# A four-batch fp32 chain of linear attention and two mixers: sign and low part of the weights by piece, the second batch's gates in the opening, the last output tile in halves

## The chip, the cores and the metric

The kernel runs on one core of a Trainium2 chip. Its engines work side by side, each through its own queue in program order: TensorE (PE, with its weight loads PEld), VectorE (DVE), ScalarE (ACT), GpSimd (POOL) and SyncE (SP), which issues nearly all DMAs. The metric is the device time of one execution in microseconds (us); lower is better. Of several runs the median is given.

## The reference

Attention with a decaying state, for 4 batches, 8 heads, 768 steps and a head dimension of 48; then a low-rank token mixer with a channel MLP; then a mixer with cosine and sine gates:

```python
f = 1.0 / (1.0 + np.exp(-f_logit))
for t in range(S):
    state = f[:, :, t, :, None] * state + einsum('bhd,bhe->bhde', k[:, :, t], v[:, :, t])
    y[:, :, t] = einsum('bhd,bhde->bhe', q[:, :, t], state)
x = y.transpose(0, 2, 1, 3).reshape(B, S, 384)
u = x + (x.transpose(0, 2, 1) @ U @ V).transpose(0, 2, 1)
x = u + np.maximum(u @ w_ch1, 0.0) @ w_ch2          # 384 -> 1536 -> 384
theta = x @ w_theta
y = einsum('ts,bsd->btd', w_tok_r, x * cos(theta)) + einsum('ts,bsd->btd', w_tok_i, x * sin(theta))
u = x + y
out = u + np.maximum(u @ w_ch, 0.0)
```

The weights come as float64 and the rest as float32.

## The kernel before

**Stages.** The program has an *opening* (about 0 to 55 us in the profile), which computes the attention of batch 0 in six chunks of 128 steps while the first weights arrive. Then `moe1(0)` runs batch 0's channel MLP, with the attention of batch 1 and the rest of the weights laid between its matmuls; `moe1(1)` and `moe1(2)` do the same with batches 2 and 3 and no more weights; `moe1(3)` is run with the conversion of the second mixer's weights; the second mixer (`theta`, `tok`, `chan`) ends the program.

**Matmuls in hi and lo.** An fp32 operand is kept as a rounded high part and the rest, and a product is three matmuls: hi by hi, hi by lo, lo by hi. `w1g(th, f)` (L630) computes 128 hidden features for one half of the tokens, nine matmuls; ScalarE then writes `hh` (L635) and VectorE `hl` (L636). `w2g(th, f)` (L647, L650) adds their product with the second weight into three PSUM banks `acc`; on a group's last feature block VectorE adds `acc` to `xT` (L655), and the next group's first `w2g` needs these banks back. In batch 0 the groups of feature blocks are `G0`: 0 to 1, 2 to 3, 4 to 7, 8 to 11, each for both token halves.

**Weights.** A weight piece is 128 x 768 numbers. It is loaded as float64 words into a buffer (`fetch`), and ScalarE's `scale` takes three steps: exponent byte (L995), sign (L998), mantissa and scale (L999). `join` (L1006) on VectorE puts them together; without `signs` VectorE takes the sign in one more operation (L1003). `w_store` then has ScalarE write the high part and GpSimd the low part (`split`, L184 and L181). The 14 pieces are numbered: 0 is U, 1 is V, then halves of w_ch1 and w_ch2 in turn (2 and 4 hold w_ch1 and 3 and 5 w_ch2 for feature blocks 0 to 3; 6 to 9 the same for 4 to 7; 10 to 13 for 8 to 11).

**Attention.** For a chunk, ScalarE takes the sigmoid of the gates (`pre_a`), VectorE runs a scan backward and one forward (`pre_s`, `pre_f`; L282, L295), and GpSimd multiplies k and q by them (L287, L299). TensorE transposes k (`kt`, L329), with a copy `ktok` on ScalarE (L331), and computes scores (`sc` in the opening, `sc4`, L384, for later batches), outputs (`xx`, copied to `xf` by ScalarE, L356) and the state (`kv`). `au` (L555) gathers the low-rank product, and on the last chunk ScalarE and VectorE make `as_` of it (L560 to L562). `first_x` and `first_h` (L591, L595) form batch 0's `u` in three PSUM banks, of which `uh` and `ul` are made.

**What sets the order.** `place` merges a list of main steps, each with a weight, with steps that have a position written as a fraction of the main list's total (1.0 and above: the first MLP stage). The positions stand in tables: `WPOS` (four steps of each weight piece: load, scale, join, store), `A1` and `A2` (the attention steps of batches 1 and 2/3), `NPOS` and `PPOS` (the second mixer's weights and first gates), `W0` (weights of the opening's steps). `KEEP` and `WARM` count matmuls on constant data (`keep_warm`, L548, 320 columns) that fill TensorE's idle time.

Of the kernel before, what the change touches and what calls it, by code (L numbers as in the profile page):

```python
# [35 lines left out]
NPOS = (
    (0.0277, 0.068, 0.0754, 0.1024),
    (0.0385, 0.1276, 0.1524, 0.178),
    (0.0319, 0.0967, 0.0975, 0.1909),
    (0.1497, 0.1976, 0.1984, 0.2572),  # L40
    (0.1837, 0.216, 0.2219, 0.2605),
    (0.234, 0.2743, 0.2753, 0.2992),
    (0.1972, 0.272, 0.2899, 0.3422),
    (0.2581, 0.3095, 0.3299, 0.3456),
    (0.2876, 0.3435, 0.36, 0.4385),
    (0.319, 0.3906, 0.3923, 0.4406),
    (0.3478, 0.4354, 0.4416, 0.4643),
    (0.3903, 0.4603, 0.4889, 0.5445),
    (0.4754, 0.5519, 0.5719, 0.5998),
    (0.4583, 0.5806, 0.5875, 0.6175),  # L50
    (0.5021, 0.5721, 0.5927, 0.6584),
    (0.5487, 0.6166, 0.6451, 0.7283),
    (0.6045, 0.66, 0.6659, 0.7498),
    (0.6183, 0.6617, 0.7209, 0.7603),
    (0.6784, 0.754, 0.7684, 0.9255),
    (0.7599, 0.7679, 0.8745, 0.9399),
    (0.7623, 0.8599, 0.8768, 0.9459),
    (0.8323, 0.9015, 0.9233, 0.9787),
    (0.9315, 0.9828, 0.9928, 1.022),
    (0.9407, 0.9937, 1.004, 1.124),  # L60
    (0.9513, 0.9992, 1.0067, 1.188),
    (1.0037, 1.0053, 1.0971, 1.1821),
    (1.0475, 1.07, 1.1124, 1.3954),
    (1.1245, 1.2045, 1.2545, 1.4229),
    (1.2775, 1.3859, 1.4334, 1.5908),
    (1.3022, 1.3332, 1.4535, 1.6135),
)
PPOS = (0.3153, 0.3907, 0.4483, 0.4725, 0.5134, 0.5728, 0.6238, 0.7426, 0.7666, 0.7963, 0.8271)
# [2 lines left out]
WPOS = (
    (0.1696, 0.231, 0.3752, 0.3979),
    (0.2201, 0.3286, 0.5165, 0.547),
    (0.2359, 0.4203, 0.7847, 0.7956),
    (0.4234, 0.6633, 0.8571, 0.9747),
    (0.2874, 0.9233, 1.0401, 1.0657),
    (0.5364, 0.9547, 1.0623, 1.1063),
    (0.4931, 1.0442, 1.1351, 1.1713),
    (0.5855, 1.1024, 1.1536, 1.2068),
    (0.7627, 1.1904, 1.2335, 1.279),  # L80
    (0.9717, 1.2212, 1.3155, 1.3293),
    (1.0728, 1.2667, 1.3516, 1.4777),
    (1.2008, 1.3522, 1.4323, 1.4924),
    (1.2548, 1.4587, 1.5342, 1.5986),
    (1.3056, 1.5483, 1.5725, 1.7332),
)
# [2 lines left out]
A1 = (
    (0.9797, 0.9861, 1.0081, 1.0804, 1.1072, 1.1676),  # L90
    (1.0384, 1.0515, 1.0971, 1.1995, 1.3043),
    (1.0862, 1.1911, 1.218, 1.3331, 1.4271),
    (1.3302, 1.348, 1.3792, 1.5171, 1.6043),
    (1.3769, 1.4457, 1.4633, 1.6201, 1.7007),
    (1.6233, 1.6281, 1.6693, 1.7973, 1.8787, 1.9131),
)
# [1125 lines left out]
```

## Time and profile before

| | us |
|---|---|
| median of 3 runs (693.7 to 695.59) | 694.93 |
| the profiled execution | 694.42 |
| its span on the core | 692.6 |
| TensorE busy | 666.1 (96%) |
| ScalarE busy | 346.9 (50%) |
| VectorE busy | 333.6 (48%) |
| GpSimd busy | 284.1 (41%) |

The rows of the trace are counted from the start of the span; the 1.8 us between span and time lie around it. A busy time is a sum over an engine's instructions in the trace. A row of the timeline gives start, duration, engine, line of the kernel, operation, tiles and shapes, and, in brackets, the idle time before it with what ended it. The granted clock is the share of full speed that TensorE was given: 1.00 is 2.4 GHz, 0.50 is 1.2 GHz.

### The profile page before, as it was taken

How to read it: one execution, taken by the hardware profiler on the slowest of the kernel's cores; microseconds unless marked ns; L12 is line 12 of the kernel's file. 1: busy time of each engine (PE TensorE's matmuls, PEld its weight loads, DVE VectorE, ACT ScalarE, POOL GpSimd, SP SyncE). 2: the span in 40 equal slices, each digit the busy share in tenths (PEclk: the TensorE clock that was granted, in tenths of full speed). 3: DMA queues.
4: the chain of work that ended last, by engine and by line, in shares of the span. 5: the costliest groups of instructions: out<-in, count | busy, mean ns of one | idle time of the engine just before them, and what ended most of it. 6: DMA issues, size and time to landing. Idle time of an engine off the chain costs nothing.

```text
span 692.6 us, 14789 instructions
## 1 busy us (share of the span) xinstructions
PE 666.1 (96%) x6196; PEld 639.5 (92%) x6196; DVE 333.6 (48%) x556; ACT 346.9 (50%) x702; POOL 284.1 (41%) x274
## 2 busy tenths in 40 slices
PE   8998989999999999999999999999999999999996
PEld 7767878998999998999999998999899999999996
DVE  7736766535534326435214678963543343343222
ACT  5868886634334234334223577766564364455321
POOL 6425757424624204534202235435572263235222
PEclk9998999999999999999999999999999999999999
DMA  9961443222222420223000444332000000000002
GB/s 243 317 194 59 131 124 101 59 59 59 58 59 72 99 61 1 59 59 81 2 1 1 128 145 138 92 115 69 2 1 35 35 0 24 35 12 13 34 24 74
DMA packets 20586, 49.79 MB, mean 72 GB/s; under 512 B 2496, under 2 KB 11200, under 8 KB 20512
## 3 DMA queue, kind: packets, MB, share of 16 engines
q1 hardware_dynamic: 20400, 48.38, 24.2%
q8 instruction: 51, 0.84, 0.5%
q10 hardware_dynamic: 112, 0.39, 0.2%
q14 instruction: 23, 0.19, 0.1%
HBM read 44.04 MB, written 4.72 MB: 70 GB/s over the span
## 4 chain that ended last, share of the span: by engine, by line
PE 67%; ACT 13%; DVE 6%; issue 5%; DMA 4%; POOL 3%; SPq 0%; POOLq 0%; ACTq 0%; DVEq 0%
PE ps_A L779 18%; PE ps_A L630 15%; PE ps_A L647 9%; PE ps_B L807 5%; PE ps_A L650 4%; PE ps_B L726 4%; DMA r<-in_wtok_dram 3%; PE ps_A L384 2%; ACT xT L998 2%; ACT w L998 1%; PE ps_B L407 1%; PE ps_B L436 1%; PE ps_B L430 1%; ACT W L184 1%; POOL W L181 1%
## 5 line engine op out<-in xcount | busy, mean ns | idle before, releaser
L636 DVE SCALAR_TENSOR_TENSOR hl<-ps_A,hh 128x384 fp32r<-128x384 f32 x96 | 53.1, 554 | 157.4 <-ACT hh L635 157.3
L779 PE MATMUL ps_A<-W,zh 128*128 128x384 f32 x576 | 125.1, 338 | 0.0
L647 PE MATMUL ps_A<-hh,W 128*128 128x384 f32 x552 | 115.8, 339 | 4.2 <-DVE xT L655 3.9
L630 PE MATMUL ps_A<-uh,W 128*128 128x384 f32 x576 | 119.2, 341 | 0.7 <-ACT uh L599 0.6
L635 ACT ACTIVATE hh<-ps_A 128x384 fp32r<-128x384 f32 x96 | 46.8, 489 | 122.8 <-PE ps_A L630 122.3
L630 PEld LDWEIGHTS ps_A<-uh,W 128*128 128x128 f32 x576 | 102.1, 191 | 2.4 <-ACT uh L599 1.1
L647 PEld LDWEIGHTS ps_A<-hh,W 128*128 128x128 f32 x552 | 96.0, 188 | 7.7 <-ACT w L995 2.9
L779 PEld LDWEIGHTS ps_A<-W,zh 128*128 128x128 f32 x576 | 100.7, 188 | 0.0
L181 POOL TENSOR_TENSOR zl<-z,zh 128x768 fp32r<-128x768 f32 x24 | 44.6, 1860 | 98.2 <-ACT zh L756 53.5
L779 PE MATMUL ps_A<-W,zl 128*128 128x384 f32 x288 | 73.3, 335 | 0.0
L630 PE MATMUL ps_A<-ul,W 128*128 128x384 f32 x288 | 66.3, 337 | 0.2 <-POOL ul L181 0.2
L650 PE MATMUL ps_A<-hl,W 128*128 128x384 f32 x276 | 65.8, 337 | 0.0
L181 POOL TENSOR_TENSOR ul<-xT,uh 128x384 fp32r<-128x384 f32 x45 | 47.1, 1060 | 42.8 <-ACT uh L580 26.4
L287 POOL TENSOR_TENSOR raw<-raw,e 112x512 f32<-112x512 f32 x24 | 32.1, 1338 | 57.4 <-DVE e L282 40.6
L630 PEld LDWEIGHTS ps_A<-ul,W 128*128 128x128 f32 x288 | 51.9, 190 | 0.7 <-POOL ul L181 0.7
L779 PEld LDWEIGHTS ps_A<-W,zl 128*128 128x128 f32 x288 | 52.1, 188 | 0.0
L650 PEld LDWEIGHTS ps_A<-hl,W 128*128 128x128 f32 x276 | 49.7, 188 | 0.1
L181 POOL TENSOR_TENSOR W<-r,W 128x384 fp32r<-128x384 f32 x24 | 27.0, 1138 | 39.9 <-ACT W L184 39.9
L732 DVE SCALAR_TENSOR_TENSOR ps_B<-kk,ps_B 128x384 f32<-128x384 f32 x24 | 13.5, 563 | 60.1 <-ACT kk L731 60.0
L181 POOL TENSOR_TENSOR xlo<-xf,xhi 128x384 fp32r<-128x384 f32 x18 | 18.3, 1014 | 58.8 <-ACT xhi L443 58.8
L299 POOL TENSOR_TENSOR raw<-raw,f 112x512 f32<-112x512 f32 x23 | 30.2, 1312 | 20.0 <-DVE f L295 17.3
L737 ACT ACTIVATE cs<-r 128x384 f32<-128x384 f32 x24 | 12.6, 525 | 42.3 <-DVE r L734 42.3
(201 smaller groups left out, 1186.4 us busy)
## 6 DMA issues: line engine op xcount, KB each, us to landing
raw<-in_qkf_dram SPq DMA_DIRECT2D x23, 576.0 KB, 5.2
r<-in_wtok_dram SPq DMA_DIRECT2D x24, 384.0 KB, 3.3
vt<-in_v_dram SPq DMA_DIRECT2D x24, 192.0 KB, 5.6
w<-in_w_dram SPq DMA_DIRECT2D x6, 768.0 KB, 8.2
xT<-in_w_dram SPq DMA_DIRECT2D x6, 768.0 KB, 5.6
out_dram<-o SPq DMA_DIRECT2D x24, 192.0 KB, 1.9
vt<-in_v_dram SPq DMA_DIRECT2D x36, 96.0 KB, 5.0
r<-in_wth_dram SPq DMA_DIRECT2D x3, 384.0 KB, 3.8
```

The source lines that it names most:

```text
L181: eng.tensor_tensor(out=out_, in0=a, in1=b, op=ALU.subtract)
L287: nc.gpsimd.tensor_tensor(out=x, in0=x, in1=e, op=ALU.mult)
L299: (nc.gpsimd if g else nc.vector).tensor_tensor(out=x, in0=x, in1=p, op=ALU.mult)
L630: mm(out=t, lhsT=w1t(lo, fb)[:, k, 128 * fo:128 * fo + 128], rhs=x[:, k], start=(n == 0), stop=(n == 8))
L635: nc.scalar.activation(out=hh, in_=t, func=ACTF.Relu)
L636: nc.vector.scalar_tensor_tensor(out=hl, in0=t, scalar=0.0, in1=f32(hh), op0=ALU.max, op1=ALU.subtract)
L647: mm(out=st["acc"][k], lhsT=w2t(lo, fb)[:, fo, 128 * k:128 * k + 128], rhs=hh, start=(first_of(f) and lo == 0), stop=False)
L650: mm(out=st["acc"][k], lhsT=w2t(0, fb)[:, fo, 128 * k:128 * k + 128], rhs=hl, start=False, stop=last_of(f))
L726: mm(out=t, lhsT=x[:, k], rhs=w[:, k], start=(n == 0), stop=(n == 8))
L779: mm(out=t, lhsT=z[:, i, 128 * k:128 * k + 128], rhs=w[:, S * i + HT * th:S * i + HT * th + HT], start=(s == 0 and n == 0), stop=(s == NCH ...
L807: mm(out=t, lhsT=w[:, k, 128 * m:128 * m + 128], rhs=x[:, k], start=(n == 0), stop=(n == 8))
L998: nc.scalar.activation(out=sign, in_=hi.bitcast(F32), func=ACTF.Copy, scale=2.0 ** -60)
```

## The change

Each weight piece gets an entry in `SIGNS`. Its lowest bit says whether ScalarE takes the sign (as before) or VectorE; the next bit puts the low part on VectorE instead of GpSimd. Pieces 2, 3, 4, 9 and 12 take their sign on VectorE, and of these 9 and 12 their low part too. Batch 1's first chunk has its gates within the opening, and its transposes and scores directly behind `first_h`, in bank A3 and A5; `first_x` uses other banks. The fillers' counts change. The last output tile is computed and stored in two halves, the second on ScalarE's DMA queue. The tables have new positions; of `NPOS`, `PPOS` and `WPOS` only some rows are shown.

```diff
-KEEP = (13, 0, 0, 2, 0, 5, 0, 0, 4, 0)
+KEEP = (14, 0, 0, 2, 1, 4, 1, 0, 5, 6)
...
-W0 = (319, 1368, 2492, 3028)
+W0 = (502, 488, 2541, 2515)
 
 WPOS = (
-    (0.1696, 0.231, 0.3752, 0.3979),
-    (0.2201, 0.3286, 0.5165, 0.547),
-    (0.2359, 0.4203, 0.7847, 0.7956),
-    (0.4234, 0.6633, 0.8571, 0.9747),
...
+    (0.1722, 0.2239, 0.3772, 0.3979),
+    (0.2231, 0.3338, 0.5249, 0.539),
+    (0.2351, 0.4172, 0.7816, 0.7925),
+    (0.4109, 0.6637, 0.8575, 1.0057),
...
 )
-VPOS = (0.7341, 0.7484)
-LN = (0, 0.0462)
+SIGNS = (1, 1, 0, 0, 0, 1, 1, 1, 1, 2, 1, 1, 2, 1)
+VPOS = (0.7318, 0.7328)
+LN = (0, 0.0416)
 A1 = (
-    (0.9797, 0.9861, 1.0081, 1.0804, 1.1072, 1.1676),
-    (1.0384, 1.0515, 1.0971, 1.1995, 1.3043),
...
+    (0.9303, 0.9452, 0.9734, 1.0007, 1.1293, 1.1657),
+    (1.0346, 1.0512, 1.0939, 1.1967, 1.3054),
...
 )
...
-            t = ps("A4" if start else "A5" if c else "B0", [128, NP, PR])
+            t = ps("A4" if start else "A5" if c else "A3" if b == 1 else "B0", [128, NP, PR])
...
-        for k, bank in enumerate(("A5", "A4", "B1")):
+        for k, bank in enumerate(("B1", "A4", "B0")):
...
-            nc.vector.scalar_tensor_tensor(
-                out=o, in0=t, scalar=0.0, in1=xT[b][:, m, HT * th:HT * th + HT], op0=ALU.max, op1=ALU.add
-            )
-            nc.sync.dma_start(out=out[b, 128 * m:128 * m + 128, HT * th:HT * th + HT], in_=o)
+            n = HT // 2 if end and (th, m) == (1, NK - 1) else HT
+            for i, eng in zip(range(0, HT, n), (nc.sync, nc.scalar)):
+                nc.vector.scalar_tensor_tensor(
+                    out=o[:, i:i + n], in0=t[:, i:i + n], scalar=0.0,
+                    in1=xT[b][:, m, HT * th + i:HT * th + i + n], op0=ALU.max, op1=ALU.add
+                )
+                eng.dma_start(out=out[b, 128 * m:128 * m + 128, HT * th + i:HT * th + i + n], in_=o[:, i:i + n])
...
-            return fetch(nc, const, src, [128, 768], nc.sync, buf=buf, signs=True)
+            return fetch(nc, const, src, [128, 768], nc.sync, buf=buf, signs=SIGNS[n] % 2 == 1)
...
-                split(hi, lo, w, lo_eng=nc.gpsimd)
+                split(hi, lo, w, lo_eng=nc.vector if SIGNS[n] // 2 % 2 else nc.gpsimd)
```

In the orders below, a row is line, operation, tiles (with buffer numbers) and shape. The changed kernel's lines are one to four higher.

ScalarE at the end of the opening, before: behind the copy `ktok` of chunk 5 come piece 4 (`w_284`), the copies `xT` and `xf`, piece 5 (`w_459`), the high part of piece 3 (`W_760`) and `as_`.

```order
L995 ACTIVATE w_284<-w_284 128x768
L998 ACTIVATE w_284<-w_284 128x768
L999 ACTIVATE w_284<-w_284 128x768
L454 ACTIVATE xT_298<-ps_A_703 128x3x128
L356 ACTIVATE xf<-ps_B_708 128x4x48
L356 ACTIVATE xf<-ps_A_709 128x4x48
L995 ACTIVATE w_459<-w_459 128x768
L998 ACTIVATE w_459<-w_459 128x768
L999 ACTIVATE w_459<-w_459 128x768
L184 ACTIVATE W_760<-w_385 128x768
L560 ACTIVATE as__84<-ps_A_398 32x384
L562 ACTIVATE as__84<-ps_A_398 32x384
```

The same place in the changed kernel:

```order
L999 ACTIVATE w_285<-w_285 128x768
L1003 ACTIVATE w_285<-w_285 128x768
L275 ACTIVATE f_73<-raw_90 112x512
L276 ACTIVATE first_79<-f_73 112x4
L277 ACTIVATE f_73<-f_73 112x4
L455 ACTIVATE xT_295<-ps_A_701 128x3x128
L357 ACTIVATE xf<-ps_B_709 128x4x48
L357 ACTIVATE xf<-ps_A_710 128x4x48
L999 ACTIVATE w_478<-w_478 128x768
L1002 ACTIVATE w_478<-w_478 128x768
L1003 ACTIVATE w_478<-w_478 128x768
L561 ACTIVATE as__84<-ps_A_396 32x384
```

Piece 4 has no sign step, batch 1's first gates (three rows) stand ahead of the copies, and the high part of piece 3 has gone behind the first `uh` and `ktok` of the next stage.

TensorE at the passage from the opening to the first MLP stage, before: the fillers (`wz`), `first_h`, one `hT` and the first `w1g`.

```order
L548 MATMUL ps_A_83<-wz 128x320 x4
L595 MATMUL ps_A_768<-vs,as__84 128x384
L595 MATMUL ps_A_770<-vs,as__84 128x384
L595 MATMUL ps_B_772<-vs,as__84 128x384
L574 MATMUL ps_B_803<-vs,as__84 128x384
L630 MATMUL ps_A_813<-uh,W_607 128x384 x3
```

And in the changed kernel:

```order
L549 MATMUL ps_A_83<-wz 128x320 x5
L596 MATMUL ps_B_767<-vs,as__84 128x384
L596 MATMUL ps_A_769<-vs,as__84 128x384
L596 MATMUL ps_B_771<-vs,as__84 128x384
L549 MATMUL ps_A_83<-wz 128x320 x6
L330 MATMUL ps_A_803<-ident,raw_90 128x112 x4
L385 MATMUL ps_A_810<-raw_90 64x64 x16
L575 MATMUL ps_B_831<-vs,as__84 128x384
L631 MATMUL ps_A_838<-uh,W_604 128x384 x3
```

Six fillers, the transposes and the scores of batch 1's first chunk now stand between `first_h` and the first `w1g`; before, transposes and scores stood three `w1g` further down.

ScalarE at piece 9 (`w_758`) in the first MLP stage, before: the piece, the `hh` behind it, and piece 10.

```order
L998 ACTIVATE w_758<-w_758 128x768
L999 ACTIVATE w_758<-w_758 128x768
L635 ACTIVATE hh<-ps_A_1128 128x384
L995 ACTIVATE w_876<-w_876 128x768
L998 ACTIVATE w_876<-w_876 128x768
```

And in the changed kernel:

```order
L999 ACTIVATE w_758<-w_758 128x768
L1003 ACTIVATE w_758<-w_758 128x768
L185 ACTIVATE W_1121<-xT_66 128x768
L636 ACTIVATE hh<-ps_A_1129 128x384
L999 ACTIVATE w_902<-w_902 128x768
```

The sign step of the piece is gone, and the high part of piece 7 stands between the piece and `hh` (before, it stood ahead of the piece).

## Rows read from the trace of the kernel before

**Rows 1.** Busy time by stretch: span; each engine busy (count); clock; DMA share; GB/s.
```profile
0.00:55.00 55.00, 48.60 (x705) 38.18 (x705) 32.79 (x51) 37.27 (x66) 23.50 (x39) 1.00 0.88 255
55.00:165.00 110.00, 102.66 (x1209) 97.11 (x1210) 62.16 (x93) 73.58 (x128) 57.01 (x49) 0.95 0.31 84
165.00:265.00 100.00, 98.54 (x1224) 95.78 (x1224) 41.17 (x65) 34.95 (x87) 36.12 (x40) 1.00 0.24 61
```

**Rows 2.** Timeline of TensorE in the opening, 19 to 57 us.
```profile
21.40 0.60 PE L329 MATMUL ps_A<-ident,raw 112*128 112x112 f32 x4 [0.55 <-ACT xT L454]
...
28.41 0.97 PE L548 MATMUL ps_A<-wz 128*128 128x320 f32 x5
...
35.65 0.86 PE L900 MATMUL ps_A<-xT,ident 128*32 128x192 f32 x16 [0.51 <-ACT xf L356]
...
55.27 0.68 PE L595 MATMUL ps_A<-vs,as__84 128*128 128x384 f32 x2 [1.98 <-ACT as__84 L562]
```

**Rows 3.** Timeline of TensorE in the first MLP stage, 57 to 135 us.
```profile
57.17 2.41 PE L630 MATMUL ps_A<-uh,W 128*128 128x384 f32 x6 [0.57 <-ACT uh L599]
...
67.37 1.15 PE L384 MATMUL ps_A<-raw 64*64 64x64 f32 x32
...
71.69 1.27 PE L647 MATMUL ps_A<-hh,W 128*128 128x384 f32 x6
...
77.61 1.05 PE L384 MATMUL ps_A<-raw 64*64 64x64 f32 x29 [1.58 <-ACT ktok L331]
...
91.85 1.45 PE L647 MATMUL ps_A<-hh,W 128*128 128x384 f32 x6 [2.59 <-DVE xT L655]
...
98.49 1.34 PE L630 MATMUL ps_A<-uh,W 128*128 128x384 f32 x6
```

**Rows 4.** Busy time by stretch, TensorE alone: span, busy (count), granted clock, DMA.
```profile
56.00:64.00 8.00, 7.43 (x27) 0.59 0.01 3
76.00:78.00 2.00, 0.42 (x15) 1.00 0.13 49
92.00:98.00 6.00, 6.00 (x122) 0.72 0.12 47
```

**Rows 5.** Timeline of ScalarE at the end of the opening.
```profile
44.28 0.55 ACT L331 ACTIVATE ktok<-ps_A 128x448 f32<-128x448 f32 x1 [1.41 <-PE ps_A L329]
44.72 0.88 ACT L995 ACTIVATE w<-w 128x768 int32<-128x768 uint8 x1
...
48.41 0.48 ACT L454 ACTIVATE xT<-ps_A 128x384 f32<-128x384 f32 x1
...
52.89 0.87 ACT L184 ACTIVATE W<-w 128x768 fp32r<-128x768 f32 x1
53.66 0.46 ACT L560 ACTIVATE as__84<-ps_A 32x384 fp32r<-32x384 f32 x1
...
55.24 0.63 ACT L274 ACTIVATE f<-raw 112x512 f32<-112x512 f32 x1
55.90 0.21 ACT L275 ACTIVATE first<-f 112x4 f32<-112x4 f32 x1
```

**Rows 6.** Timeline of ScalarE in the first MLP stage, at piece 9.
```profile
87.33 1.96 ACT L998 ACTIVATE w<-w 128x768 f16<-128x768 f32 x1
...
90.13 0.52 ACT L635 ACTIVATE hh<-ps_A 128x384 fp32r<-128x384 f32 x1
```

**Rows 7.** Timelines of VectorE and GpSimd at two joins.
```profile
35.60 1.77 DVE L1006 SCALAR_TENSOR_TENSOR w<-w 128x768 int32<-128x768 int32 x1
...
67.56 0.93 DVE L1006 SCALAR_TENSOR_TENSOR w<-w 128x768 int32<-128x768 int32 x1
...
35.27 1.28 POOL L299 TENSOR_TENSOR raw<-raw,f 112x512 f32<-112x512 f32 x1
```

**Rows 8.** Timeline of VectorE at the last output tile, and at a narrower operation.
```profile
687.06 0.56 DVE L813 SCALAR_TENSOR_TENSOR o<-ps_B,xT 128x384 f32<-128x384 f32 x1 [1.01 <-PE ps_B L807]
...
17.38 0.36 DVE L369 TENSOR_TENSOR kvs<-ps_A,kvs 112x192 f32<-112x192 f32 x1 [0.68 <-PE ps_A L365]
```

More of the change, by code (lines that the diff above doesn't have):

```diff
@@ L34 @@
 WARM = 28
-KEEP = (13, 0, 0, 2, 0, 5, 0, 0, 4, 0)
+KEEP = (14, 0, 0, 2, 1, 4, 1, 0, 5, 6)
 NPOS = (
-    (0.0277, 0.068, 0.0754, 0.1024),
+    (0.0277, 0.068, 0.0754, 0.1016),
     (0.0385, 0.1276, 0.1524, 0.178),
[L39 to L48, printed above, removed]
+    (0.0118, 0.0761, 0.0774, 0.1647),
+    (0.1316, 0.1795, 0.1817, 0.2391),
+    (0.1571, 0.1929, 0.1988, 0.2401),
+    (0.22, 0.2559, 0.2569, 0.2808),
+    (0.1977, 0.2725, 0.2904, 0.3432),
+    (0.2587, 0.3101, 0.3305, 0.3518),
+    (0.2822, 0.3381, 0.3546, 0.4333),
+    (0.3198, 0.3902, 0.3931, 0.4329),
+    (0.3521, 0.4397, 0.4459, 0.4686),
+    (0.366, 0.452, 0.4872, 0.5445),
@@ L49 @@
     (0.4754, 0.5519, 0.5719, 0.5998),
-    (0.4583, 0.5806, 0.5875, 0.6175),
-    (0.5021, 0.5721, 0.5927, 0.6584),
-    (0.5487, 0.6166, 0.6451, 0.7283),
+    (0.454, 0.5806, 0.5875, 0.6175),
+    (0.4999, 0.5699, 0.5905, 0.6562),
+    (0.5487, 0.6166, 0.6451, 0.7314),
     (0.6045, 0.66, 0.6659, 0.7498),
-    (0.6183, 0.6617, 0.7209, 0.7603),
-    (0.6784, 0.754, 0.7684, 0.9255),
+    (0.6183, 0.6698, 0.7209, 0.7603),
+    (0.6784, 0.7611, 0.7684, 0.9255),
     (0.7599, 0.7679, 0.8745, 0.9399),
-    (0.7623, 0.8599, 0.8768, 0.9459),
@@ L58 @@
[L58 removed]
+    (0.7708, 0.8609, 0.8768, 0.9459),
+    (0.8323, 0.8833, 0.9233, 0.9783),
     (0.9315, 0.9828, 0.9928, 1.022),
[L60 to L66, printed above, removed]
[L67 to L68 removed]
@@ L69 @@
-W0 = (319, 1368, 2492, 3028)
+    (0.9407, 0.9943, 0.9952, 1.124),
+    (0.95, 0.9979, 1.0054, 1.1867),
+    (1.0045, 1.012, 1.0994, 1.19),
+    (1.0481, 1.0706, 1.1127, 1.3942),
+    (1.138, 1.218, 1.268, 1.4361),
+    (1.2752, 1.3771, 1.4246, 1.582),
+    (1.2995, 1.341, 1.4508, 1.6108),
+)
+PPOS = (0.3186, 0.3907, 0.458, 0.4826, 0.5474, 0.5735, 0.6305, 0.7134, 0.764, 0.7928, 0.8256)
+W0 = (502, 488, 2541, 2515)
 WPOS = (
-    (0.1696, 0.231, 0.3752, 0.3979),
-    (0.2201, 0.3286, 0.5165, 0.547),
-    (0.2359, 0.4203, 0.7847, 0.7956),
-    (0.4234, 0.6633, 0.8571, 0.9747),
[L76 to L85, printed above, removed]
-)
@@ L87 @@
-VPOS = (0.7341, 0.7484)
-LN = (0, 0.0462)
+    (0.1722, 0.2239, 0.3772, 0.3979),
+    (0.2231, 0.3338, 0.5249, 0.539),
+    (0.2351, 0.4172, 0.7816, 0.7925),
+    (0.4109, 0.6637, 0.8575, 1.0057),
+    (0.2906, 0.9233, 1.0401, 1.0658),
+    (0.5412, 0.9562, 1.0641, 1.1042),
+    (0.5028, 1.0539, 1.1715, 1.1815),
+    (0.5981, 1.115, 1.1706, 1.2215),
+    (0.7624, 1.1918, 1.2349, 1.2668),
+    (0.9671, 1.2179, 1.3088, 1.314),
+    (1.071, 1.2626, 1.3501, 1.4314),
+    (1.2016, 1.3587, 1.4386, 1.4989),
@@ L89 @@
+    (1.2541, 1.4688, 1.5388, 1.6034),
+    (1.3043, 1.5463, 1.57, 1.7325),
+)
+SIGNS = (1, 1, 0, 0, 0, 1, 1, 1, 1, 2, 1, 1, 2, 1)
+VPOS = (0.7318, 0.7328)
+LN = (0, 0.0416)
 A1 = (
-    (0.9797, 0.9861, 1.0081, 1.0804, 1.1072, 1.1676),
-    (1.0384, 1.0515, 1.0971, 1.1995, 1.3043),
[L92 to L95, printed above, removed]
+    (0.9303, 0.9452, 0.9734, 1.0007, 1.1293, 1.1657),
+    (1.0346, 1.0512, 1.0939, 1.1967, 1.3054),
+    (1.1556, 1.1844, 1.2231, 1.3565, 1.4328),
+    (1.3232, 1.3447, 1.3772, 1.5026, 1.6038),
+    (1.3889, 1.447, 1.4497, 1.6499, 1.7031),
+    (1.6306, 1.6529, 1.6766, 1.8067, 1.8864, 1.9349),
@@ L864, in w_issue @@
             if j == "U":
-                return fetch(nc, const, U, [128, NCH * RANK], nc.sync, buf=buf, signs=True)
+                return fetch(nc, const, U, [128, NCH * RANK], nc.sync, buf=buf, signs=SIGNS[n] % 2 == 1)
             if j == "V":
-                return fetch(nc, const, [V[:, i:i + S // 4] for i in range(0, S, S // 4)], [128, S // 4], nc.sync, buf=buf, signs=True)
+                return fetch(nc, const, [V[:, i:i + S // 4] for i in range(0, S, S // 4)], [128, S // 4], nc.sync, buf=buf, signs=SIGNS[n] % 2 == 1)
             sl = slice(768 * h, 768 * h + 768)
             src = w1[j].rearrange("p (k f) -> p k f", k=NK)[:, :, 256 * h:256 * h + 256] if j < 3 else w2[j - 3][:, sl]
-            return fetch(nc, const, src, [128, 768], nc.sync, buf=buf, signs=True)
+            return fetch(nc, const, src, [128, 768], nc.sync, buf=buf, signs=SIGNS[n] % 2 == 1)
         def w_store(n, w):
```

## Prediction

> **What bounds the kernel now.** I read the busy times by stage first. The batch whose weights are still being converted takes 55 to 165 us, TensorE busy for 102.66 of 110; the next batch does the same matmuls (1224 records against 1209) in 100 us [rows 1]. So some 10 us of the first stage are lost, and the opening ahead of it (0 to 55) has ScalarE busy 37.27 of 55. That next stage keeps TensorE at 98.54 of 100, and the change does not aim at it or at the later ones. Next I read what TensorE waited for. In the opening it waits little, in pieces: 0.55 and 0.51 us for ScalarE copies, and then 1.98 for `as_` [rows 2]. In the first stage: 0.57, 1.58, 2.59 [rows 3]. Then the clock: after the 1.98 the granted clock is 0.59 on average from 56 to 64 (half rate, 1.2 GHz, for most of it), after the 2.59 it is 0.72 from 92 to 98; after the 1.58 it stayed at 1.00 [rows 4]. That is 8 x 0.41 = 3.3 us and 6 x 0.28 = 1.7 us of lost matmul time. Behind all three waits stands ScalarE's queue, which runs in program order: one weight piece holds it for 3.7 us (44.72 to 48.41), and `as_` at 53.66 stands behind two such pieces and one store [rows 5]; the `hh` that the 2.59 waits for (by way of VectorE) stands behind piece 9's 1.96 us sign step [rows 6].
>
> **The change, part by part.**
>
> *Signs.* Pieces 2, 3, 4, 9 and 12 lose their ScalarE sign step: five at 1.96 [rows 6], 9.8 us off ScalarE. Each puts one more VectorE join of the same shape in its place: 0.93 us where GpSimd is idle at its start [rows 7]. The price has two ends: the join that starts at 35.60 while GpSimd is in a multiply of 1.28 that began at 35.27 takes 1.77 [rows 7]. So 5 x 0.93 = 4.7 to 5 x 1.77 = 8.9 us on VectorE. Pieces 9 and 12 also move their low part there; no row shows that shape on VectorE. The nearest is the same join, also 768 elements a partition read from two SBUF inputs, 0.93 to 1.77. I take 0.93, since the GpSimd work that it replaces is gone too. In the opening, pieces 2 and 3 are covered: their extra joins stand before a mask that TensorE needs at about 38 and that is ready near 37.
>
> Here a rule speaks against the change. Those two rows show a VectorE join started 0.33 us into a GpSimd operation and ending 0.82 us (1.77 + 35.60 - 35.27 - 1.28) after it, about its own length [rows 7]. The Trainium skill (SBUF — State Buffer, section Who interferes with whom) says that a VectorE `tensor_tensor` with both inputs in SBUF contends with GpSimd's reads, and that whoever issues second fully blocks. The trace agrees (0.82 against 0.93). By that rule every added join would cost its full length plus what is left of the GpSimd operation: the VectorE rival below.
>
> *A, the opening up to `first_h` (55.27).* TensorE: five idle-filling groups ahead of `xx(5)` lose one matmul of 0.97 / 5 = 0.19 us: 1.0 us. The 0.55 wait goes, because the copy now stands ahead of V's conversion, and the 0.51 wait goes, since its copy stood behind piece 3. That is 2.1 us, and by this `ktok` of chunk 5 comes at 42.2 instead of 44.28 [rows 2, 5]. From there ScalarE alone sets the end. Before, from `ktok` to `as_` it runs 53.66 - 44.28 = 9.4 us. Now piece 4's sign goes (-1.96), the weight store moves behind (-0.8, from 52.89 to 53.66), and the second batch's gates come in (0.63 and two steps of 0.21, +1.05) [rows 5]: 7.7. So `as_` starts at 49.9, and `first_h`, 1.6 behind it as before, at 51.5 to 51.7: **A = -3.6**. Its ends are -2.0 (only TensorE's share and nothing of ScalarE's) and -4.5 (some pieces still overlap better). VectorE and GpSimd have nothing else to do for the gates after 46; the covers are there. TensorE's wait before `first_h` shrinks from 1.98 to about 0.4 and the six fillers behind it follow on at once, so I expect no clock drop at 56.
>
> *B, from `first_h` to 71.69* (the matmul that starts the second token half's sum). After `first_h` stand 6 fillers (1.2), the moved transposes (0.60) and scores (1.15) [rows 2, 3]; the first `w1g` then starts 4 us after `first_h`, against 1.9 before, but at full clock, and the transposes and scores are gone from further down. On matmuls alone this would save the whole 3.3. ScalarE does not allow it: between `first_h` and the `hh` of 71.69 it has the three `uh` copies, three `xT` copies, the new `ktok`, two weight stores, three `uh`, two `hh`, one set of gates and piece 6 with its sign (3.7), 14 us of work and about 1.5 us of waits, and VectorE's two steps behind `hh` take 1. That is 16 us against 16.4 before: **B = -0.4** (0 to -1.2). TensorE then waits some 1.7 us there, a new wait of the old kind.
>
> *C, from 71.69 to 98.49.* Piece 9 without its sign brings `hh` 1.96 us earlier; one more store in front of it takes back 0.9: -1.0 on the 2.59. If that wait is short enough, the second clock drop goes too: -1.7. Against it, `ktok` of chunk 1 now stands behind gates as well (1.58 becomes 1.8), and `ktok` of chunk 2 stands behind piece 10, with its sign, while TensorE comes to it earlier: +1.0. **C = -1.5** (-3.0 to +1.5).
>
> *The last output tile.* VectorE's step of 0.56 [rows 8] becomes two of 192 elements. The nearest row of that width takes 0.36 [rows 8], so the first half leaves 0.2 earlier, the second ends up to 0.16 later, and each transfer is half as large, on two queues. **-0.2** (+0.2 to -0.5). ScalarE has nothing left to do there.
>
> *The rest costs nothing.* The banks of `first_x` are free by then (the gates' bank and `xx`'s, which `xf` has emptied). Bank A3 for the moved transposes is `w1g`'s own first bank, so its copy must be done before the first matmul: by my count it is, with about 0.2 us to spare. The reordered loads of `wth` and `wtok` and the later batches' new places shift steps by less than a tile among stages where TensorE is at 98%: 0, within 1 us. On SP's queue the raw loads now stand behind piece 13; its buffer is free before they are due.
>
> Sum: -3.6 - 0.4 - 1.5 - 0.2 = -5.7 against the profiled execution's 694.42 (span 692.6 and 1.8 around it): 688.7. The median of the runs, 694.93, lies 0.5 above that execution, so I forecast **689.2**.
>
> **The rivals.**
>
> *Given back.* The first stage is bound by ScalarE's conversions rather than by when it starts, so A is eaten by longer waits at 71.69 and 91.85. For it: ScalarE is busy 73.58 of 110 in the stage [rows 1], the most of any stage, and all of its long waits end on it; against it: five sign steps are gone, two of them in the stage. It gives -5.7 + 3.6 = -2.1, 692.8. Chance 0.15.
>
> *VectorE takes ScalarE's place.* In the stage VectorE gets piece 4's join, and two operations each for pieces 9 and 12, and `hl` and the sums queue behind them. If all five stand in TensorE's way and are lengthened by GpSimd: 0.93 to 1.77 each, 4.7 to 8.9 us, of which slack takes some half: +3.5, 692.7. For it: rows 7; against it: VectorE is busy only 62.16 of 110 [rows 1]. Chance 0.10. By the Trainium skill's rule (SBUF — State Buffer, Who interferes with whom), this is what happens wherever GpSimd is reading.
>
> *Slower: the clock.* My count leaves four waits of 1.3 to 1.8 us between 66 and 91. Waits of 1.98 and 2.59 were each followed by half rate, one of 1.58 was not [rows 3, 4]. If these four all bring it down, at (3.3 + 1.7) / 2 = 2.5 each, that is +10 on -5.7: +4.3, 699.2; it turns to the slower side from the third drop on. Against it: busy matmuls lie between them, and they are nearer to 1.58. Chance 0.07.
>
> *Better.* The waits of B and C are shorter than I count and the lost 10 us come back almost whole: -8.5, 686.4. Chance 0.08. That the signs do not move is excluded by the listed order.
>
> **How the numbers follow.** The forecast (687 to 691, one clock drop among its mishaps) gets 0.60. Faster by over 0.3% (2.1 us, about what a measurement of this kernel can tell from no change): forecast, better, and half of the two rivals near 692.8: 0.60 + 0.08 + 0.12 = 0.80. Within 0.3%: the other halves, 0.13. Slower: 0.07. The range runs from 685.7 (the better ends of A, B, C and the tail, -0.9 - 0.8 - 1.5 - 0.3 = -3.5) to 693.0, which takes in both rivals near 692.8 for the most part; outside are the clock rival and the tails.
>
> **What would show it.** Right: `first_h` near 51.6; granted clock 1.00 at 56 to 64; no sign step (the 1.95 us activation) for five pieces; the matmul of 71.69 near 67.7 and that of 98.49 near 93; later stages as long as before. Wrong: `first_h` later than 53.5 (A); clock below 0.9 in more than one place before 100 (C); VectorE's joins at 1.8 us with TensorE waiting for `hl` or the sums.

## The result, and the profile after

The changed kernel takes **685.58 us** (median of 4 runs, 683.78 to 686.65) against 695.09 (median of 4) of the kernel before in the same comparison: ratio 0.9864, interval 0.9838 to 0.9889. Measured again beside the last experiments it took 684.06 against 694.33 (ratio 0.9852, 0.9834 to 0.9869). It is faster, as forecast, but by 9.5 to 10.3 us instead of 5.7, and 685.58 lies 0.1 us below the lower end of the range.

The profiled execution took 683.78 (span 682.0) against 694.42 (span 692.6). Busy time by stretch, the counterpart of [rows 1]; the columns are the same:

```profile
0.00:55.00 55.00, 50.74 (x724) 40.45 (x726) 38.42 (x59) 34.92 (x72) 25.10 (x41) 1.00 0.89 256
55.00:165.00 110.00, 104.31 (x1267) 99.33 (x1264) 68.58 (x100) 70.71 (x129) 58.11 (x50) 1.00 0.31 84
165.00:265.00 100.00, 98.37 (x1224) 95.61 (x1223) 41.89 (x66) 35.27 (x87) 35.68 (x40) 1.00 0.24 61
```

In the stretch from 55 to 165 us TensorE has 1267 records instead of 1209, the granted clock is 1.00 instead of 0.95, ScalarE has 2.9 us less to do and VectorE 6.4 more. TensorE's timeline, with the matmuls of [rows 2, 3] (line numbers are one to four higher now):

```profile
52.25 0.44 PE L596 MATMUL ps_B<-vs,as__84 128*128 128x384 f32 x1 [0.40 <-ACT as__84 L563]
...
56.02 1.20 PE L631 MATMUL ps_A<-uh,W 128*128 128x384 f32 x6
...
68.06 1.46 PE L648 MATMUL ps_A<-hh,W 128*128 128x384 f32 x6 [1.35 <-ACT hh L636]
...
73.75 1.05 PE L385 MATMUL ps_A<-raw 64*64 64x64 f32 x29 [1.14 <-ACT ktok L332]
...
85.77 1.45 PE L648 MATMUL ps_A<-hh,W 128*128 128x384 f32 x6 [0.38 <-DVE xT L656]
...
90.08 1.05 PE L385 MATMUL ps_A<-raw 64*64 64x64 f32 x29 [1.01 <-ACT ktok L332]
...
92.08 1.31 PE L631 MATMUL ps_A<-uh,W 128*128 128x384 f32 x6
```

The waits of 1.98 and 2.59 are down to 0.40 and 0.38. What is left is 1.35, 1.14 and 1.01, each for a ScalarE result, and no lower clock follows any of them. ScalarE at the end of the opening, against [rows 5]:

```profile
43.05 0.54 ACT L332 ACTIVATE ktok<-ps_A 128x448 f32<-128x448 f32 x1 [1.09 <-PE ps_A L330]
...
45.07 0.62 ACT L275 ACTIVATE f<-raw 112x512 f32<-112x512 f32 x1
...
47.89 1.92 ACT L1002 ACTIVATE w<-w 128x768 f16<-128x768 f32 x1
...
50.64 0.46 ACT L561 ACTIVATE as__84<-ps_A 32x384 fp32r<-32x384 f32 x1
```

Piece 4 is two steps long, the gates stand behind it, piece 5 still has its sign (47.89), and `as_` starts at 50.64 instead of 53.66. Around piece 9, against [rows 6], the store of piece 7 stood ahead of the piece before (first row) and stands behind it now (second row):

```profile
85.59 0.91 ACT L184 ACTIVATE W<-xT 128x768 fp32r<-128x768 f32 x1
```
```profile
83.24 0.95 ACT L185 ACTIVATE W<-xT 128x768 fp32r<-128x768 f32 x1
```

Either way it lies between the same two `hh`. These start 4.9 us apart before (85.22 and 90.13) and 2.8 apart now (81.29 and 84.04). The price on VectorE, three of the five added joins (line 1007) and the two low parts that it took over:

```profile
34.64 1.76 DVE L1007 SCALAR_TENSOR_TENSOR w<-w 128x768 int32<-128x768 int32 x1
...
40.41 0.95 DVE L1007 SCALAR_TENSOR_TENSOR w<-w 128x768 int32<-128x768 int32 x1
...
90.27 1.59 DVE L1007 SCALAR_TENSOR_TENSOR w<-w 128x768 int32<-128x768 int32 x1
...
94.11 1.18 DVE L182 TENSOR_TENSOR W<-w,W 128x768 fp32r<-128x768 f32 x1 [0.98 <-ACT W L185]
...
118.80 0.95 DVE L182 TENSOR_TENSOR W<-xT,W 128x768 fp32r<-128x768 f32 x1
```

The other two take 0.95 each, so the five cost 6.2 us, inside the bounds of 4.7 and 8.9. The last tile's two halves take 0.62 together against 0.56:

```profile
676.53 0.62 DVE L816 SCALAR_TENSOR_TENSOR o<-ps_B,xT 128x192 f32<-128x192 f32 x2 [1.01 <-PE ps_B L808]
```

**Where the 10.6 us of span went.** The same matmuls compared in the two traces, start against start:

| stretch (us of before) | forecast | measured | from which starts |
|---|---|---|---|
| A, to `first_h` | -3.6 | -3.0 | 55.27, now 52.25 |
| B, to 71.69 | -0.4 | -0.6 | 71.69, now 68.06 |
| C, to 98.49 | -1.5 | -2.8 | 98.49, now 92.08 |
| rest of the first MLP stage, to 171.46 | 0 | -2.1 | 171.46, now 162.99 |
| 171 to 412 | 0 | 0.0 | 412.80, now 404.33 |
| 412 to 481, second mixer's weights converted | 0 | -2.1 | 481.17, now 470.62 |
| from there to the end | -0.2 | -0.1 | spans 692.6 and 682.0 |

The two rows of -2.1 were forecast at 0. In part they are waits that the trace of before does show. These are four of them, on TensorE:

```profile
106.86 1.33 PE L647 MATMUL ps_A<-hh,W 128*128 128x384 f32 x6 [0.27 <-ACT hh L635]
...
120.70 1.46 PE L647 MATMUL ps_A<-hh,W 128*128 128x384 f32 x6 [0.39 <-DVE xT L655]
...
127.94 1.05 PE L384 MATMUL ps_A<-raw 64*64 64x64 f32 x29 [0.82 <-ACT ktok L331]
...
425.45 0.79 PE L726 MATMUL ps_B<-thhi,x2hi 128*128 128x384 f32 x3 [0.62 <-ACT x2hi L184]
```

After the change, the counterpart of the last has no wait. The first row here is the matmul that ends the first stage (171.46 before):

```profile
162.99 1.31 PE L631 MATMUL ps_A<-uh,W 128*128 128x384 f32 x6
...
415.34 0.68 PE L727 MATMUL ps_B<-thhi,x2hi 128*128 128x384 f32 x3
```

The listed waits are not all of it. Between 98.49 and 129.94 of before 2.3 us are won, of which 0.27, 0.20, 0.39 and 0.82 were waits; 0.2 is lost again by 171.46. Between 412.80 and 425.45 1.6 us are won, of which 0.62 was a wait; the rest lies in matmuls that follow each other more slowly without a listed wait. The six on `hh` at 414.59, for example, take 1.51 us to the next ones, and 1.04 after the change.

### The profile page after: what moved, and what is told of

The parts are those of the page before. It is cut to its first block, busy times and chain, and to the rows that moved or that the text cites. A ratio compares the mean times of both kernels' runs of the same rounds, so it can differ in the third digit from the quotient of the medians.

```text
span 682.0 us, 14794 instructions
## 1 busy us (share of the span) xinstructions
PE 661.0 (97%) x6198; PEld 637.1 (93%) x6198; DVE 338.6 (50%) x564; ACT 337.5 (49%) x697; POOL 280.5 (41%) x272
## 4 chain that ended last, share of the span: by engine, by line
PE 76%; ACT 9%; issue 5%; DVE 4%; POOL 4%; DMA 3%; SPq 0%; DVEq 0%; POOLq 0%; ACTq 0%
PE ps_A L780 18%; PE ps_A L631 17%; PE ps_A L648 11%; PE ps_B L808 6%; PE ps_A L651 5%; PE ps_B L727 4%; PE ps_A L385 3%; POOL W L182 2%; DMA r<-in_wtok_dram 2%; PE ps_B L408 2%; PE ps_B L431 1%; PE ps_B L437 1%; PE ps_A L330 1%; PE ps_A L454 1%; DMA raw<-in_qkf_dram 1%
## 5 line engine op out<-in xcount | busy, mean ns | idle before, releaser
L631 PE MATMUL ps_A<-uh,W 128*128 128x384 f32 x576 | 117.2, 337 | 1.2 <-ACT xT L455 1.0
L631 PEld LDWEIGHTS ps_A<-uh,W 128*128 128x128 f32 x576 | 100.6, 188 | 2.5 <-ACT xT L455 1.2
L182 POOL TENSOR_TENSOR ul<-xT,uh 128x384 fp32r<-128x384 f32 x45 | 46.7, 1054 | 42.2 <-ACT uh L581 25.9
```

What stands on the lines that cost most here:

```text
L182: eng.tensor_tensor(out=out_, in0=a, in1=b, op=ALU.subtract)
L631: mm(out=t, lhsT=w1t(lo, fb)[:, k, 128 * fo:128 * fo + 128], rhs=x[:, k], start=(n == 0), stop=(n == 8))
```

## The experiments

All times are medians, beside the kernel before on the same chip. Where a difference is below 1 us I go by the traces, matmul start against matmul start, since the medians' intervals are 2 us wide. The theory: ScalarE's queue order sets the waits up to 98 us, so the sign steps carry most of the gain, and the places of the work behind 98 us carry the rest. The rivals: the places alone carry it; the clock and its filling matmuls carry it; VectorE takes ScalarE's place.

**The control.** The changed kernel unedited.

> The changed kernel itself once more, beside the two that follow, so that differences of 1 us can be told. If the spread between profiles of the same instructions (opening 0.3 to 0.9 later than in the first profile in every run that shares it, and a wait of 0.9 or 1.85 near 422 us) belongs to the kernel and not to the edits, this profile lies 0.3 to 1.9 above the first one's 683.78, and the median at 685.0 to 686.3.

684.06, profile and median. Two rows of its TensorE timeline:

```profile
51.05 0.45 PE L596 MATMUL ps_B<-vs,as__84 128*128 128x384 f32 x1 [0.40 <-ACT as__84 L563]
...
421.61 0.61 PE L648 MATMUL ps_A<-hh,W 128*128 128x384 f32 x2 [1.84 <-DVE xT L656]
```

The profile lies 0.3 above the first one, the least that was expected, and the median below the expected range. Two differences nearly cancel: `first_h` came 1.2 us earlier than in the first profile, and the wait near 422 is 1.84 instead of 0.90, which gives most of it back. In ten profiles whose opening has the same instructions `first_h` starts between 51.05 and 53.28, on average at 52.4 (55.27 and 55.74 in two of the kernel before). So A is -3.1, and one profile can miss it by 1 us. In all ten `as_` starts 7.6 us behind `ktok` of chunk 5; what moves is `ktok`, between 41.84 and 44.07, on average at 43.2. What moves it was not followed further. A difference of a median below 1.5 us is therefore no verdict here.

**Signs back on ScalarE, all else as changed.**

```diff
-SIGNS = (1, 1, 0, 0, 0, 1, 1, 1, 1, 2, 1, 1, 2, 1)
+SIGNS = (1, 1, 1, 1, 1, 1, 1, 1, 1, 1, 1, 1, 1, 1)
```

> The changed kernel with the sign step of all 14 pieces back on ScalarE and every low part on GpSimd; all places, fillers and banks as changed. Theory, the five sign steps carry the first stage: as_ about 2.0 later, first_h about 2.0 later, the waits for hh and ktok longer by up to 2.0 each, one clock drop back: 685.6 + 5 = 690.6 (689 to 693). Rival, the new places carry it and ScalarE had slack: under 1 us, 686.5.

692.03 (ratio 0.9958, 0.9946 to 0.9971): without the signs 6.5 to 7.4 us of the gain are gone, inside the expected range but more than the 5 in its middle. `first_h` comes 4.4 later than the average above, not 2.0. Of this, 2.4 lie ahead of `ktok`, where pieces 2 and 3 have their sign step back, and 2.0 behind it, piece 4's: `as_` is 9.65 behind `ktok`, not 7.6. (This is one profile, so the 2.4 can be off by 1.)

```profile
45.59 0.54 ACT L332 ACTIVATE ktok<-ps_A 128x448 f32<-128x448 f32 x1 [1.41 <-PE ps_A L330]
...
55.24 0.46 ACT L561 ACTIVATE as__84<-ps_A 32x384 fp32r<-32x384 f32 x1
```
```profile
56.84 0.44 PE L596 MATMUL ps_B<-vs,as__84 128*128 128x384 f32 x1 [1.12 <-ACT as__84 L563]
...
92.49 1.46 PE L648 MATMUL ps_A<-hh,W 128*128 128x384 f32 x6 [2.55 <-DVE xT L656]
```

The expected clock drop did not come (see the last section). Between 98 and 172 us this kernel still gains 1.7 on the one before, and that is without any sign moved: most of the -2.1 there comes from the places. With the signs alone (the next run) it is 0.7.

**Signs alone, in the kernel before.** `SIGNS` as in the change, and its two uses; nothing else.

> The kernel before (695.1) with the new signs and low parts alone; its own places, fillers and banks. Theory, the signs carry the gain of the first stage by themselves: as_ and the 2.59 wait each 2.0 earlier, at least the second clock drop gone: 695.1 - 5 = 690. Rival, the signs need the new places, since VectorE's added joins now stand in front of hl and the sums: 694 to 696. The two edits' shares need not add up; the sum of this gain and of what the changed kernel loses without its signs, against 9.5, shows by how much they depend on each other.

690.89 (0.9943, 0.9927 to 0.9959): -3.8, between theory and rival. The wait that was 1.98 is 1.23 and the one that was 2.59 is 2.21:

```profile
53.61 0.61 PE L596 MATMUL ps_A<-vs,as__84 128*128 128x384 f32 x2 [1.23 <-ACT as__84 L563]
...
89.13 1.85 PE L648 MATMUL ps_A<-hh,W 128*128 128x384 f32 x6 [2.21 <-DVE xT L656]
```

Both are still followed by a lower clock (0.80 from 56 to 64 us, 0.75 from 88 to 92). So the signs bring 3.8 alone and 6.5 to 7.4 together with the places: the two depend on each other.

**The opening's signs alone.**

```diff
-SIGNS = (1, 1, 0, 0, 0, 1, 1, 1, 1, 2, 1, 1, 2, 1)
+SIGNS = (1, 1, 0, 0, 0, 1, 1, 1, 1, 1, 1, 1, 1, 1)
```

> The changed kernel with the signs of pieces 9 and 12 back on ScalarE and their low parts on GpSimd; pieces 2, 3 and 4 stay as changed. Theory, these two carry what the first stage gained behind 85 us: the wait for hh at 85.77 grows from 0.38 by up to 1.96, and piece 12 gives back part of the 2.1 between 98 and 163 us: 685.6 + 3 = 688.6 (687.5 to 690.5), nothing changed up to 80 us. Rival, the opening's three carry all of it and later waits only move: 685.6 to 686.5.

688.07 (0.9901, 0.9886 to 0.9916), as the theory had it. Nothing changes up to 80 us, then piece 9's sign brings the wait back, and the clock falls:

```profile
87.81 2.26 PE L648 MATMUL ps_A<-hh,W 128*128 128x384 f32 x6 [2.49 <-DVE xT L656]
```
```profile
88.00:92.00 4.00, 4.00 (x43) 3.74 (x46) 1.06 (x3) 3.97 (x6) 2.21 (x3) 0.65 0.51 159
```

By 98 us that costs 2.1, about the length of that one sign step [rows 6]; by 172 us it is 2.5, with piece 12's. This profile then loses another 2.3 near 425, at a wait and a clock drop that the last section shows; the median's loss of 2.5 agrees with the first stage's.

**Low parts of pieces 9 and 12 on GpSimd** (`2` becomes `0` in `SIGNS`).

> The changed kernel with the low parts of pieces 9 and 12 back on GpSimd (their signs stay on VectorE). Theory, the low part on VectorE (1.18 and 0.95 in the trace against 1.86 on GpSimd) only spares GpSimd, which TensorE does not wait for: 685.6, within 0.7. Rival, GpSimd is behind there, and the two of 1.86 make the first matmuls on piece 12's weights or the next scores late: 686.5 to 688.

684.93 (0.9872, 0.9854 to 0.9889): no difference; up to 404 us every matmul is 0.3 later than in the first profile, as much as `first_h` is. That part of the change is worth nothing that can be measured.

**The filling matmuls of before.**

```diff
-KEEP = (14, 0, 0, 2, 1, 4, 1, 0, 5, 6)
+KEEP = (13, 0, 0, 2, 0, 5, 0, 0, 4, 0)
```

> The changed kernel with the idle-filling matmuls of the kernel before (13, 0, 0, 2, 0, 5, 0, 0, 4, 0), so none behind first_h. Theory of the prediction, the six behind first_h are what keeps the granted clock at 1.00 there: a wait of about 0.4 + 1.2 comes back behind first_h, and the clock falls for some us: 685.6 + 2.5 = 688 (687 to 689). Rival, the clock stays up because the wait for as_ is short, and the fillers only lie in waits: 685.6, within 0.5, clock 1.00 at 56 to 64 us.

685.2 (0.9871, 0.9854 to 0.9888): the rival. The wait comes back, behind `first_h`, and the clock does not fall (window 56 to 64 us, clock in the third column from the right):

```profile
54.08 1.15 PE L385 MATMUL ps_A<-raw 64*64 64x64 f32 x32 [1.21 <-POOL raw L300]
```
```profile
56.00:64.00 8.00, 7.82 (x43) 7.09 (x42) 5.46 (x8) 6.06 (x10) 4.96 (x4) 1.00 0.00 0
```

`first_h` starts at 51.69 here, in the early half of the spread above, and not 1.0 late, so the fewer fillers of the opening do not show their 1.0 us either, as far as one profile tells.

**The second batch's gates, scores and transposes at their old places.**

```diff
-    (0.9303, 0.9452, 0.9734, 1.0007, 1.1293, 1.1657),
+    (0.9797, 0.9861, 1.0081, 1.0804, 1.1072, 1.1676),
...
-"A5" if c else "A3" if b == 1 else "B0"
+"A5" if c else "B0"
```

> The changed kernel with the second batch's first gates, scores and transposes at their places of before (and their bank). Theory, the moved 1.75 us of TensorE work fill a time in which it would wait anyway, so taking them back loses them on the path, and ktok of that chunk is waited for again near 75 us: 685.6 + 1.5 = 687.1 (686.5 to 688). Rival, the moved gates hold ScalarE 1.05 us ahead of as_, and their return brings first_h forward by that: 685 or less.

689.26 (0.9925, 0.9906 to 0.9943): 3.7 slower than the changed kernel's 685.58, more than twice what the theory gave. `first_h` is not earlier (52.81). Behind it and the six fillers TensorE has nothing to do, and a second wait stands near 78:

```profile
57.48 0.44 PE L575 MATMUL ps_B<-vs,as__84 128*128 128x384 f32 x1 [3.00 <-ACT xT L603]
...
77.70 1.05 PE L385 MATMUL ps_A<-raw 64*64 64x64 f32 x29 [2.03 <-ACT ktok L332]
```

Both are followed by a lower clock (0.79 from 56 to 64 us and from 76 to 84). The fillers stand behind `first_h` in this run and the clock falls; in the run before it they are gone and the clock stays up. So the moved work, and not the fillers, keeps the clock up there in the changed kernel. But this work is more than TensorE's. The gates are back on ScalarE between `as_` and the `uh` copies:

```profile
53.17 0.62 ACT L275 ACTIVATE f<-raw 112x512 f32<-112x512 f32 x1
```

The last `xT` copy, for which TensorE waits, starts 4.1 us behind `first_h` here (56.94) and 2.5 in the changed kernel (54.77). So some 1.6 of the 3.00 go with the gates' place on ScalarE; the shares of gates, scores and transposes in the 3.7 were not separated.

**The second mixer's places**, once the old ones in the changed kernel, once the new ones in the kernel before (tables `NPOS` and `PPOS` exchanged).

> The changed kernel (685.6) with the second mixer's weights loaded and converted at the places of the kernel before (both tables of that stage). Theory, the new places there are worth what the traces show between 412 and 481 us, 2.1: 687.7, the 0.62 wait for x2hi back at about 416 us, all matmuls up to 404 us unchanged, those after 471 us later by 2.1. Rival, the 2.1 came from the state in which that stage begins (earlier loads, other buffers free): 685.6, within 0.5, and no such wait.

> The kernel before (694.9) with the changed kernel's places for the second mixer's weights alone. Theory, these places are worth 2.0 by themselves, as the changed kernel lost 2.0 in its trace between 404 and 482 us with the old ones: 692.9, all matmuls up to 404 us where they were, those after 482 us 2.0 earlier. Rival, they fit only the changed kernel's state, as the run with all signs back on ScalarE had them and gained only 0.6 there: 694.3 to 695.

686.02 (0.9875, 0.9861 to 0.9889) and 693.53 (0.9988, 0.9972 to 1.0003). The medians move by 0.4 (against 685.58) and 1.3 (against 694.82), which decides nothing; the traces do. With the old places the changed kernel gains nothing on the one before between 412 and 481 us (7.52 ahead at the one, 7.60 at the other), and the wait for `x2hi` is back:

```profile
418.05 0.79 PE L727 MATMUL ps_B<-thhi,x2hi 128*128 128x384 f32 x3 [0.75 <-ACT x2hi L185]
```

With the new places the kernel before gains 1.8 there and nothing up to 412. So the new places carry this part, 1.8 to 2.1 in these pairs, less another 0.9 in those executions (the control is one) in which the wait near 422 is 1.84. Over all fourteen profiles with the new places this stretch gains between -0.3 and 2.2 on the first profile of the kernel before, on average 1.4; the two others with the old places gain 0.1 and 0.0.

**The last tile in one step.**

```diff
-            n = HT // 2 if end and (th, m) == (1, NK - 1) else HT
+            n = HT
```

> The changed kernel with the last output tile in one step and one transfer again. Theory, the halves are worth what the two traces show behind the last matmul, under 0.1: 685.6, span from the last matmul to the end within 0.15 of the changed kernel's. Rival, as the prediction had it, 0.2 and up to 0.5: 685.8 to 686.1, the transfer of 192 KB landing later by that much.

685.32 (0.9878, 0.986 to 0.9896): the medians can't tell. The traces lean one way, taken together: from the first matmul of the last output tile to the end of the span it is 7.57 us here, and 7.35, 7.46 and 7.51 in the three profiles of kernels with the old tail (the kernel before and its two variants); in the thirteen with halves it is 7.24 to 7.68, median 7.30. That points to -0.2, the prediction's term, and not to the 0.1 of my first reading, but the two groups overlap, and four profiles against thirteen do not settle it.

**One more sign on VectorE: piece 10.**

```diff
-SIGNS = (1, 1, 0, 0, 0, 1, 1, 1, 1, 2, 1, 1, 2, 1)
+SIGNS = (1, 1, 0, 0, 0, 1, 1, 1, 1, 2, 0, 1, 2, 1)
```

> The changed kernel with the sign of piece 10 alone on VectorE too. Theory, the wait of 1.01 for ktok at 90.08 goes: 685.6 - 0.9 = 684.7, matmuls up to 85 us unchanged. Rival, the added join stands before the sums that the same place waits for next: 685.6 to 686.5. Together with the run of three signs it shows whether the shares add up.

685.84 (0.9882, 0.9868 to 0.9897): no gain. The wait of 1.01 at 90.08 is gone and 1.2 us are won by 92; then 1.9 are lost:

```profile
101.25 0.79 PE L651 MATMUL ps_A<-hl,W 128*128 128x384 f32 x3 [0.97 <-DVE hl L637]
...
104.03 1.08 PE L385 MATMUL ps_A<-raw 64*64 64x64 f32 x29 [0.68 <-POOL raw L300]
```

In front of that `hl` on VectorE stand the added join and the one behind it, which meets a GpSimd product of 1.87 that began at 97.44:

```profile
98.19 1.93 DVE L1010 SCALAR_TENSOR_TENSOR w<-w 128x768 int32<-128x768 int32 x1
```

**Three more: 6, 7 and 10** (those three at 0).

> The changed kernel with the signs of pieces 6, 7 and 10 on VectorE too. Theory, ScalarE's queue still sets the three waits of 1.35 (68.06), 1.14 (73.75) and 1.01 (90.08), each behind one such piece: without the signs they shrink by most of 3.5, less what VectorE's three added joins (0.93 to 1.77) put in front of hl and the sums: 685.6 - 2 = 683.6 (682.3 to 685). Rival, VectorE becomes the engine waited for in the first stage: 686 to 688, with waits for hl or the sums of xT in place of those for hh and ktok.

685.92 (0.9885, 0.9871 to 0.9899): the median is the changed kernel's, with the rival's waits (in a profile of 688.48, the slowest of the four executions). Those for `hh` and `ktok` are gone; in their place stand 0.88 for the sums of `xT`, 0.98 for a later `hh` and 0.97 for `hl`.

**The same with joins moved.** Piece 10's joins right behind piece 9's (`WPOS[10][2]` from 1.3501 to 1.3095), with piece 10 alone; then also piece 7's behind the sums (`WPOS[7][2]` from 1.1706 to 1.2), with pieces 6, 7 and 10.

> The changed kernel with piece 10's sign on VectorE, as in the run that gained 1.2 by 91 us and lost 1.9 behind it, but with that piece's two joins moved up, to stand right behind piece 9's, in a time in which VectorE waited. Theory, what was lost there came from the place (the joins stood in front of hl, and beside a GpSimd product): the waits of 0.97 for hl and 0.68 behind it go, and the gain stays: 685.6 - 0.9 = 684.7. Rival, VectorE has no room for a further join in that stage wherever it stands: 685.6 to 686.5, and the wait turns up elsewhere.

> The run of three further signs (6, 7, 10), with piece 10's joins moved up as in the run before this, and piece 7's joins moved behind the three sums of xT, the scan, the mask and hl. Theory, as there, the place decides: the three waits for hh and ktok stay gone, and the waits of 0.88 for the sums and 0.97 for hl go: 685.6 - 2 = 683.6 (682.5 to 684.8). Rival, VectorE is full in that stage: 685.6 to 687.

684.71 (0.9867, 0.9848 to 0.9885) and 685.3 (0.9873, 0.9857 to 0.989), against 684.06 of the control beside them: neither is faster. The waits that were to go went, so the place does matter, but others came. First kernel, then second:

```profile
96.08 1.46 PE L648 MATMUL ps_A<-hh,W 128*128 128x384 f32 x6 [0.68 <-DVE xT L656]
```
```profile
86.96 1.46 PE L648 MATMUL ps_A<-hh,W 128*128 128x384 f32 x6 [2.17 <-DVE xT L656]
```

Both times TensorE now waits for VectorE's sums. I read this as two engines close to balance with five signs moved; no version here beats the changed kernel.

**All signs of the MLP pieces on VectorE** (5, 6, 7, 8, 10, 11, 13 at 0 as well).

> The changed kernel with the signs of all twelve MLP weight pieces on VectorE (seven more: 5, 6, 7, 8, 10, 11, 13). Theory, the sign's place matters at the pieces ahead of a wait alone, and VectorE (62 of 110 us busy in that stage before) has room: as with three more signs, 683.6, within 1. Rival, the prediction's: VectorE takes ScalarE's place, seven joins of 0.93 to 1.77 (6.5 to 12.4 us) lie in front of hl and the sums: 687 to 690.

694.86 (1.0015, 1.0005 to 1.0025): the whole gain is lost, and more than the rival asked for. TensorE waits for VectorE, directly and through a ScalarE store that needs a join, and the clock falls at both waits (0.79 from 68 to 76 us, 0.72 from 88 to 96 and 0.71 from 96 to 100), which is some 5 us of the loss:

```profile
70.39 1.84 PE L648 MATMUL ps_A<-hh,W 128*128 128x384 f32 x6 [4.17 <-DVE xT L656]
...
92.60 2.26 PE L648 MATMUL ps_A<-hh,W 128*128 128x384 f32 x6 [3.58 <-ACT W L185]
```

One join (VectorE) takes 3.88 us beside two operations of GpSimd:

```profile
65.43 3.88 DVE L1010 SCALAR_TENSOR_TENSOR w<-w 128x768 int32<-128x768 int32 x1
```
```profile
64.68 1.86 POOL L288 TENSOR_TENSOR raw<-raw,e 112x512 f32<-112x512 f32 x1 [2.08 <-issue]
66.50 0.20 POOL L289 TENSOR_TENSOR pend<-first,e 112x4 f32<-112x4 f32 x1
66.66 1.83 POOL L182 TENSOR_TENSOR W<-w,W 128x768 fp32r<-128x768 f32 x1
```

## Why the prediction was right or wrong

- **What bounds it, and the direction**: right. The clock is 1.00 at 56 to 64 us, the 2.59 is 0.38, five pieces have no sign step, `first_h` and the matmul of 71.69 lie within 0.7 us of the forecast in the first profile.
- **A** (-3.0, and -3.1 on average, for -3.6): the ScalarE half was right, 7.6 us from `ktok` to `as_` for the 7.7 booked. The half ahead of `ktok` was not: on average it came at 43.2, not at 42.2. The fillers' 1.0 us in that half do not show (with the old ones `first_h` stays in the spread), while the signs of pieces 2 and 3 are worth 2.4 ahead of `ktok` with the new places, where the term booked only the 0.51 wait behind piece 3.
- **B**: right in size (-0.6 for -0.4), and the limit that it named is there, a wait of 1.35 for `hh` where it counted 1.7. But it gave the moved gates, scores and transposes no price of their own; putting them back costs 3.7, with waits of 3.00 and 2.03 and a lower clock behind each. The reason given for the clock, six fillers that follow on at once, fell: without them it stays at 1.00 over a wait of 1.21.
- **C** was mis-sized, -2.8 for -1.5. Piece 9's sign brought the wait down by 2.2 where I booked 1.0. I had charged 0.9 for a store in front of that `hh`, but the store stood in front of it before as well, ahead of the piece (85.59); the two `hh` came 2.2 closer. The `ktok` wait that was to grow to 1.8 fell to 1.14. The clock drop did go (-1.7 booked; the rows from 91.85 to 98.49 show 1.3 of it), and the new wait for the third `ktok` was right (+1.0, measured 1.01). The run with the opening's signs alone shows 2.1 of it hanging on this one step.
- **"The rest costs nothing ... 0, within 1 us"** is the step that failed. What it put at nothing was worth 4.1 in the first profile: 2.1 between 98 and 172 us, of which 1.7 is there with every sign back on ScalarE, and 2.1 in the second mixer (1.4 on average over the profiles), where exchanging two tables takes it away (2.0) and gives 1.8 to the kernel before. The sign "later stages as long as before" failed with it. For 98 to 172 us the sum had no term at all: C ended at 98.49, and this is still the first stage, at 93% in [rows 1]. For the mixer I read TensorE's share of 98% and did not look for waits in the places whose tables the change rewrites; the trace of before shows some of them. Which table moved the first 2.1 was not separated. The runs rule out some: with the old fillers, the old first row of `A1`, the old mixer tables, or the low parts on GpSimd it is still 2.0 to 2.1, so among what acts in that stretch the other rows of `A1` and the rows of `WPOS` remain, with a few tenths for piece 12's sign (1.7 without it).
- **The last tile**: nothing speaks against it. The two profiles compared above give -0.1, all seventeen point to -0.2, with overlap.
- **VectorE takes ScalarE's place** did not happen with five signs, and did with twelve: 694.86, past the 692.7 of the rival. Three further signs bring nothing. For twelve, some 5 us of the loss is the clock, which the rival did not count. The rule behind the rival (the Trainium skill, SBUF — State Buffer, section Who interferes with whom) agrees with the rows: the 3.88 us join ends 0.82 after the last GpSimd operation, about its own length of 0.93. Its order by issue does not: that last GpSimd operation began 1.23 us after the join and went first.
- **Given back** did not happen: what `first_h` gained (3.0) is still there at 71.69 (3.6) and at 91.85 (6.1).
- **The clock rival** did not happen: the waits of 1.35, 1.14 and 1.01 never brought the clock down, in this profile or the control.
- **Better** (686.4) came nearest in the number, but its reason, shorter waits in B and C, gives only 1.5 of the 4.9 us that the profile gained beyond the sum.
